# Result chains of a seven-product stage spread over successive slots, and two outputs of the last group taken together

## Chip, cores and metric

The kernel runs on one core of one Trainium2 chip. The core has TensorE (PE, matrix products), VectorE (DVE), ScalarE (ACT), GpSimd (POOL) and SyncE (SP, which only issues DMAs here), each with a queue of its own that it works through in order. The metric is the device time in microseconds of one execution; lower is better.

## The reference, cut to what matters

An attention layer with mixing of heads before and after the softmax feeds two multilayer blocks on 1792 tokens of width 768. The stages that matter here, called layers one to four:

```python
a = x @ w1                       # layer one, 768 -> 1024
b = x @ w2
y = (a * b @ w3) @ w_out         # layer two; the kernel multiplies by w3 @ w_out, 1024 -> 768
h = np.maximum(y @ w_in, 0.0)    # layer three, 768 -> 2048
out = h * h @ w_out2             # layer four, 2048 -> 768
```

## The kernel before, in words

The tokens are worked in two halves of 896, each half as two tiles t = 0, 1 of 448 tokens. Every float32 operand is split in a high and a low part, and each product is three matmuls (high by high, high by low, low by high; `mm3`, line 60). So every weight piece is prepared by ACT (`wh`, the rounded copy, line 117) and then by POOL (`wl`, the rest, line 145), and every activation by ACT (`...h`, line 711) and then DVE (`...l`, line 712).

All weight pieces form one list, and `stage(s, run)` is one slot of it. In slot s it issues, in this order: the DMA of a later piece, sums of weights for a piece further on (`combine`, DVE), `wh` of piece s+3, `wl` of piece s+2, then whatever earlier slots left in the list `late`, and then `run`, which is the matmuls of piece s and the work on their result. The program order of every engine is the order of these calls; nothing reorders it later. SP runs ahead of the others and waits only for the four buffers `raw`/`quad` of weights. What stands in `late[0]` is issued in the next slot, in `late[1]` in the one after, and so on.

In the second half of the tokens, layers one and three work two output blocks of 128 and both tiles together as one "quad": seven products of half depth instead of eight, in seven slots of nine matmuls each (`quad`, `l1_quad`, `l3_quad`). Four of the weight pieces are sums and differences, made by `combine` 1 to 4 (tiles S1 to S4). The products go to four PSUM banks A to D, some added onto an older result, in the order A, B, C, A, B, C, D. In slot 0 ACT copies A (`s1`); in slot 1 DVE adds `u2`; in slot 2 ACT copies C (`s5`). The four results (r, t) come out in slots 3 to 6: (0,0) by ACT's Relu in slot 3; (1,1) in slot 4, where DVE adds `u3` and then POOL adds u3 and s5; (0,1) in slot 5 and (1,0) in slot 6, added by DVE. Each result of layer three is then squared (DVE), rounded (ACT) and its rest taken (DVE): the "result chain". Quad j makes blocks 2j and 2j+1 of h.

Layer three and four alternate in the second half: quads 0, 1, 2, part 0, quads 3, 4, part 1, quads 5, 6, part 2, quad 7, part 3. A part gr of layer four (`l4_part`) multiplies blocks 4gr to 4gr+3 of h with the weights of the six outputs e = 0 to 5, one weight piece (one slot) for each output, 24 matmuls per slot, so that part 3 alone needs the results of the quad just ahead of it. Quad 7 (`end`) and the last quad of layer one use DVE in place of POOL for result (1,1).

In the tables below a matmul of layer four reads `l<-h_0h,wl` (tile 0, high part, low weights), and the suffixes of `qh4D` say quad 4 of layer three, bank D.

Of the kernel before, what the change touches and what calls it, by code (L numbers as in the profile page):

```python
# [14 lines left out]
ALU = mybir.AluOpType  # L15
# [22 lines left out]
def fused_kernel(ctx, tc, q, k, v, w_pre, w_post, w1, w2, w3t, wo, win, wo2, eye, out):  # L38
# [492 lines left out]
    class Moe:  # L531
        def __init__(self, pre):
            self.w = Weights(None, pre, PW, 4, 2, 3, 8, 8)
            self.wp, self.pre = None, pre
            self.xy, self.late, self.acc, self.ready = {}, [[] for _ in range(4)], {}, set()
            self.units, self.wot = [], {}
            for hf in range(2):
# [17 lines left out]
                if hf == 0:  # L555
                    for gr in range(2):
                        self.units += [self.l3(hf, 8 * gr + f) for f in range(8)]
                        self.units += [self.l4(hf, gr, e) for e in range(6)]
                else:
                    for gr in range(4):  # L560
                        js = range(2 * gr + (gr > 0), min(2 * gr + 3, 8))
                        self.units += [self.l3_quad(j) for j in js]
                        self.units += [self.l4_part(gr, e) for e in range(6)]
# [13 lines left out]
        def stage(self, s, run=None):  # L577
# [7 lines left out]
            if quad(s + 5) and self.pieces[s + 5][2] == ("S", 2, 0):  # L585
                w.combine(quad(s + 5), 1)
                w.combine(quad(s + 5), 2)
            if quad(s + 3):
                _, q, name = self.pieces[s + 3]
                if name[0] == "S" and name[1] > 2:  # L590
                    w.combine(q, name[1])
                w.ft[s + 3] = q.f[name]
                w.place(s + 3)
                w.high(s + 3)
# [228 lines left out]
        def l1_quad(self, j, second):  # L823
            end = j == 3

            def done(r, t, x, y=None):
# [10 lines left out]
                p = self.tile(f"p1_{m}_{t}")  # L837
                if y is not None:
                    self.add(p, x, y, eng)
                    x = p  # L840
                mul = lambda: nc.vector.tensor_tensor(p, x, self.xy["a", m, t], ALU.mult)
                if eng is nc.gpsimd:
                    self.late[0].append(mul)
                    self.split_late(ab, p, 1, 2)
                else:
                    mul()
                    self.split_late(ab, p, 0, 0 if end else 1)
# [4 lines left out]
        def l3_quad(self, j):  # L852
            end = j == 7

            def done(r, t, x, y=None):
                f = 2 * j + r
                eng = nc.gpsimd if r and t and not end else nc.vector
                hb = self.xy["h", 1, f, t] = self.pair(f"h1_{f}_{t}")
                p = self.tile(f"h21_{f}_{t}")
                if y is None:  # L860
                    nc.scalar.activation(p, x, AF.Relu)
                    nc.vector.tensor_tensor(p, p, p, ALU.mult)
                    self.split_late(hb, p)
                    return
                self.add(p, x, y, eng)
                square = lambda: nc.vector.scalar_tensor_tensor(p, p, 0.0, p, ALU.max, ALU.mult)
                if eng is nc.gpsimd:
                    self.late[0].append(square)
                    self.split_late(hb, p, 1, 2)
                else:  # L870
                    square()
                    self.split_late(hb, p, 0, 0 if end else 1)
# [120 lines left out]
        def l4_part(self, gr, e):  # L993
            def run(ws, _):
                accs = [self.psum(f"l41_{gr}_{e}_{t}") for t in range(2)]
                term = lambda c, t: (self.chunk(ws, c), self.xy["h", 1, 4 * gr + c, t])
                for cs, order in (((0, 1), (0, 1)), ((2,), (0, 1)), ((3,), (1, 0))):
                    for t in order:
                        mm3(accs[t], [term(c, t) for c in cs], cs[0] == 0, cs[0] == 3)
                for t, acc in enumerate(accs):  # L1000
# [11 lines left out]
            return [(wo2d[e, :, PW * gr : PW * gr + PW], False)], run  # L1012
# [123 lines left out]
```

## Time and profile before

| | us |
|---|---|
| median of 3 runs | 1320.99 (1317.67 to 1323.35) |
| profiled execution, its own time | 1316.99 |
| its span in the profile | 1314.9 |
| PE busy | 1274.1 (97%) |
| DVE busy | 835.6 (64%) |
| ACT busy | 707.1 (54%) |
| POOL busy | 528.3 (40%) |

The span runs from the first to the last recorded work; the device time has about 2 us more around it. PE is close to always busy, so the time that can be taken away without taking away matmuls is the little in which PE issues none or issues them slowly. Matmuls overlap, so idle time understates a stop: the distance from one start to the next is the safer measure. A share of busy time averages over stages; the rows below are from the stages that the change touches, from 900 us on.

### The profile page before, as it was taken

Reading aid. Unit: us, or ns where it says so; the run is one execution under the profiler, and the core shown is the slowest. Engines: PE = TensorE matmul, PEld = TensorE weight load, DVE = VectorE, ACT = ScalarE, POOL = GpSimd, SP = SyncE. Lnnn points to the kernel's source line nnn. Section 1 sums busy time; section 2 is a strip of 40 time slices with the busy share of each in tenths; the row PEclk is TensorE's granted clock in tenths of the full one; section 3 lists DMA queues with packets and bytes.
Section 4 is the critical chain, followed back from the end, with each engine's and each line's share of the span. In section 5 each row is a group of like instructions: output and inputs, shape, how many; then the busy total and the mean of one; then the engine's idle time right before and its main releaser. Section 6 shows DMA issues by size and latency. Waiting matters only on the chain.

```text
span 1314.9 us, 23201 instructions
## 1 busy us (share of the span) xinstructions
PE 1274.1 (97%) x8470; PEld 1096.2 (83%) x8470; DVE 835.6 (64%) x1520; ACT 707.1 (54%) x1565; POOL 528.3 (40%) x572
## 2 busy tenths in 40 slices
PE   7999999999998999999999999999999999999998
PEld 3667777776766798999999999999999998889897
DVE  5888888889788686543127734769666337364733
ACT  5988889888886565443225533544344334341420
POOL 4354265245324512002222322237676456453631
PEclk9999999999999999999999999999999999999999
DMA  6666476566566577654135744683221111211312
GB/s 216 167 179 190 132 202 207 140 186 202 143 176 195 159 218 224 218 157 150 65 93 156 209 159 131 177 293 122 80 73 57 61 52 44 77 47 52 87 32 84
DMA packets 105158, 184.50 MB, mean 140 GB/s; under 512 B 21589, under 2 KB 72789, under 8 KB 104533
## 3 DMA queue, kind: packets, MB, share of 16 engines
q1 hardware_dynamic: 84624, 160.40, 41.3%
q10 hardware_dynamic: 20421, 22.63, 4.8%
q8 instruction: 67, 1.10, 0.3%
q14 instruction: 46, 0.38, 0.1%
HBM read 111.43 MB, written 33.03 MB: 110 GB/s over the span
## 4 chain that ended last, share of the span: by engine, by line
PE 76%; DVE 6%; issue 6%; POOL 5%; DMA 4%; ACT 2%; SPq 0%; POOLq 0%; ACTq 0%; DVEq 0%
PE l L60 32%; PE sp L318 8%; PE y L60 7%; PE tp L383 5%; PE p L60 5%; PE pv L435 5%; POOL wl L145 4%; PE sc L292 4%; DMA r<-s 2%; DVE pl L374 2%; DMA kraw<-k 1%; DVE nm L324 1%; DVE p L397 1%; ACT ph L358 0%; DMA raw<-wo2d 0%
## 5 line engine op out<-in xcount | busy, mean ns | idle before, releaser
L145 POOL TENSOR_TENSOR wl<-f,wh 128x384 fp32r<-128x384 f32 (+1 forms) x88 | 101.0, 1149 | 309.7 <-ACT wh L117 299.6
L318 PE MATMUL sp<-r,kpre 120*120 120x448 f32 x360 | 159.2, 562 | 11.4 <-ACT p L332 7.3
L332 ACT ACTIVATE p<-sp,nm 120x448 f32<-120x448 f32 x180 | 113.8, 644 | 49.6 <-DVE nm L324 49.5
L374 DVE SCALAR_TENSOR_TENSOR pl<-p,sm,ph 120x448 f16<-120x448 f32 (+3 forms) x270 | 136.9, 561 | 0.0
L324 DVE TENSOR_REDUCE nm<-sp 120x1 f32<-120x448 f32 x180 | 107.7, 619 | 41.7 <-PE sp L318 37.4
L383 PEld LDWEIGHTS <-ph 120*128 120x128 f16 x1260 | 92.9, 98 | 31.6 <-issue 23.8
L101 DVE TENSOR_SCALAR f<-y 128x384 int32<-128x384 int32 (+1 forms) x120 | 82.5, 688 | 55.5 <-ACT y L89 53.6
L358 ACT ACTIVATE ph<-p,sm 120x448 f16<-120x448 f32 (+1 forms) x180 | 108.0, 666 | 16.8 <-DVE sm L352 12.6
L383 PE MATMUL tp<-kwh,ph 120*128 120x120 f16 x630 | 106.0, 217 | 4.8 <-DVE p L399 2.2
L347 POOL TENSOR_SCALAR sm<-sm 120x2 f32<-120x2 f32 (+3 forms) x94 | 25.0, 266 | 204.1 <-ACT p L332 200.1
L318 PEld LDWEIGHTS sp<-r,kpre 120*120 120x120 f32 x360 | 58.1, 183 | 56.3 <-issue 20.9
L383 PE MATMUL tp<-kwh,pl 120*128 120x120 f16 x630 | 105.1, 216 | 0.0
L383 PE MATMUL tp<-kwl,ph 120*128 120x120 f16 x630 | 105.1, 216 | 0.0
L292 PE MATMUL sc<-kt,qh 128*110 128x448 f32 (+1 forms) x192 | 98.2, 512 | 2.3 <-DVE kt L256 1.5
L303 ACT ACTIVATE s<-sc 110x448 f32<-110x448 f32 (+1 forms) x186 | 90.8, 561 | 5.5 <-PE sc L292 5.1
L145 POOL TENSOR_TENSOR wl<-raw,wh 128x512 fp32r<-128x512 f32 x48 | 66.4, 1392 | 50.8 <-ACT wh L117 50.2
L103 DVE SCALAR_TENSOR_TENSOR f<-raw,f 128x384 int32<-128x384 int32 (+1 forms) x120 | 81.4, 678 | 4.1
L117 ACT ACTIVATE wh<-f 128x384 fp32r<-128x384 f32 (+1 forms) x104 | 58.3, 561 | 43.5 <-DVE f L103 36.7
L435 PE MATMUL pv<-p,v 128*64 128x110 f32 (+1 forms) x1536 | 81.0, 262 | 0.6 <-ACT xs L445 0.6
L435 PEld LDWEIGHTS pv<-p,v 128*64 128x64 f32 x1536 | 74.1, 137 | 4.0 <-ACT xs L445 0.9
L60 PE MATMUL l<-h_0h,wl 128*128 128x448 f32 x192 | 70.0, 364 | 5.5 <-POOL wl L145 5.5
L397 DVE TENSOR_SCALAR p<-tp,iv 128x360 f32<-128x360 f32 x135 | 74.2, 578 | 1.3 <-PE tp L383 1.3
(1372 smaller groups left out, 3681.8 us busy)
## 6 DMA issues: line engine op xcount, KB each, us to landing
r<-s SPq DMA_DIRECT2D x172, 210.0 KB
raw<-w SPq DMA_DIRECT2D x32, 384.0 KB
raw<-win SPq DMA_DIRECT2D x32, 384.0 KB
raw<-wo SPq DMA_DIRECT2D x24, 512.0 KB
kraw<-k SPq DMA_DIRECT2D x24, 448.0 KB
raw<-w3t SPq DMA_DIRECT2D x16, 512.0 KB
qraw<-q SPq DMA_DIRECT2D x35, 220.0 KB
v<-v SPq DMA_DIRECT2D x4, 1536.0 KB
```

The costliest lines, as they stand in the source:

```text
L60: nc.tensor.matmul(acc, w, x, start=(first and i == 0 and j == 0), stop=(last and i == n - 1 and j == 2), skip_group_check=again,)
L145: eng.tensor_tensor(self.out[i][1], self.ft.pop(i), f32(self.out[i][0]), ALU.subtract)
L292: nc.tensor.matmul(sc[:ic], t[:, hh * ic : hh * ic + ic], self.kt[b, h // 2][:, h % 2], start=(i == 0), stop=(i == 1))
L303: nc.scalar.activation(self.st[n][:ic, h], self.sc.pop((n, h))[:ic], AF.Copy)
L318: nc.tensor.matmul(t[:kk], self.kpre[:kk, :kk], self.rt.pop(g)[:kk], start=True, stop=True)
L324: nc.vector.tensor_reduce(nm[:kk], self.sp[g][:kk], AX.X, ALU.max, negate=True)
L332: nc.scalar.activation(p[:kk], self.sp.pop(g)[:kk], AF.Exp, bias=self.nm.pop(g)[:kk], accum_out=self.sm[g // 2][:kk, g % 2 : g % 2 + 1],)
L358: nc.scalar.activation(h[:, to], p[:, fr], AF.Copy, scale=sm)
L374: nc.vector.scalar_tensor_tensor(l[:, to], p[:, fr], sm, h[:, to], ALU.mult, ALU.subtract)
L383: nc.tensor.matmul(t[:, j], p[:, at : at + 128], w, start=(i == 0), stop=(i == 2))
L397: nc.vector.tensor_scalar(d, t[:, main], self.iv, None, ALU.mult)
L435: nc.tensor.matmul(t[64 * e : 64 * e + 64, x, :w], self.v[b][:, j, g], self.p2[n][:, j * NH + g, :w], start=(j == 0), stop=(j == JC - 1),)
```

## The change

Four edits. The sums S3 and S4 of every quad are issued one slot earlier, in the slot ahead of the one in which ACT first reads them. The result chains are cut into links that are issued in successive slots: for the result (1,1) that POOL adds, the addition, the product or square, the rounding and the rest stand in the next slot and the three after it; for the other results of layer three outside the last quad, square, rounding and rest follow one slot apart; result (0,0) is cut so in the last quad too. And in part 3 the first two outputs of layer four form one unit of two slots: nothing is multiplied in the first, both are multiplied in the second, going through the blocks of h in the outer loop and the outputs in the inner one.

```diff
--- before.py
+++ after.py
@@ -532,7 +532,7 @@
         def __init__(self, pre):
             self.w = Weights(None, pre, PW, 4, 2, 3, 8, 8)
             self.wp, self.pre = None, pre
-            self.xy, self.late, self.acc, self.ready = {}, [[] for _ in range(4)], {}, set()
+            self.xy, self.late, self.acc, self.ready = {}, [[] for _ in range(5)], {}, set()
             self.units, self.wot = [], {}
             for hf in range(2):
                 if hf == 0:
@@ -560,7 +560,8 @@
                     for gr in range(4):
                         js = range(2 * gr + (gr > 0), min(2 * gr + 3, 8))
                         self.units += [self.l3_quad(j) for j in js]
-                        self.units += [self.l4_part(gr, e) for e in range(6)]
+                        es = [(e,) for e in range(6)] if gr < 3 else [(0, 1), (2,), (3,), (4,), (5,)]
+                        self.units += [self.l4_part(gr, x) for x in es]
             kept = [u[2] if len(u) > 2 else None for u in self.units]
             self.units = [u[:2] for u in self.units]
             self.pieces = [s for ss, _ in self.units for s in ss]
@@ -585,10 +586,10 @@
             if quad(s + 5) and self.pieces[s + 5][2] == ("S", 2, 0):
                 w.combine(quad(s + 5), 1)
                 w.combine(quad(s + 5), 2)
+            if quad(s + 4) and self.pieces[s + 4][2] in (("S", 3, 0), ("S", 4, 0)):
+                w.combine(quad(s + 4), self.pieces[s + 4][2][1])
             if quad(s + 3):
                 _, q, name = self.pieces[s + 3]
-                if name[0] == "S" and name[1] > 2:
-                    w.combine(q, name[1])
                 w.ft[s + 3] = q.f[name]
                 w.place(s + 3)
                 w.high(s + 3)
@@ -835,16 +836,16 @@
                     return
                 ab = self.xy["ab", 1, m, t] = self.pair(f"ab1_{m}_{t}")
                 p = self.tile(f"p1_{m}_{t}")
+                mul = lambda: nc.vector.tensor_tensor(p, x if y is None else p, self.xy["a", m, t], ALU.mult)
+                if eng is nc.gpsimd:
+                    self.late[0].append(lambda: self.add(p, x, y, eng))
+                    self.late[1].append(mul)
+                    self.split_late(ab, p, 2, 3)
+                    return
                 if y is not None:
-                    self.add(p, x, y, eng)
-                    x = p
-                mul = lambda: nc.vector.tensor_tensor(p, x, self.xy["a", m, t], ALU.mult)
-                if eng is nc.gpsimd:
-                    self.late[0].append(mul)
-                    self.split_late(ab, p, 1, 2)
-                else:
-                    mul()
-                    self.split_late(ab, p, 0, 0 if end else 1)
+                    self.add(p, x, y)
+                mul()
+                self.split_late(ab, p, 0, 0 if end else 1)
 
             src = [w12d[int(second), 2 * j + r] for r in range(2)]
             return self.quad(f"{j}{int(second)}", src, lambda: self.xq, 3, done)
@@ -854,22 +855,25 @@
 
             def done(r, t, x, y=None):
                 f = 2 * j + r
-                eng = nc.gpsimd if r and t and not end else nc.vector
                 hb = self.xy["h", 1, f, t] = self.pair(f"h1_{f}_{t}")
                 p = self.tile(f"h21_{f}_{t}")
+                square = lambda: nc.vector.scalar_tensor_tensor(p, p, 0.0, p, ALU.max, ALU.mult)
                 if y is None:
                     nc.scalar.activation(p, x, AF.Relu)
-                    nc.vector.tensor_tensor(p, p, p, ALU.mult)
-                    self.split_late(hb, p)
-                    return
-                self.add(p, x, y, eng)
-                square = lambda: nc.vector.scalar_tensor_tensor(p, p, 0.0, p, ALU.max, ALU.mult)
-                if eng is nc.gpsimd:
+                    self.late[0].append(lambda: nc.vector.tensor_tensor(p, p, p, ALU.mult))
+                    self.split_late(hb, p, 1, 2)
+                elif end:
+                    self.add(p, x, y)
+                    square()
+                    self.split_late(hb, p, 0, 0)
+                elif r and t:
+                    self.late[0].append(lambda: self.add(p, x, y, nc.gpsimd))
+                    self.late[1].append(square)
+                    self.split_late(hb, p, 2, 3)
+                else:
+                    self.add(p, x, y)
                     self.late[0].append(square)
                     self.split_late(hb, p, 1, 2)
-                else:
-                    square()
-                    self.split_late(hb, p, 0, 0 if end else 1)
 
             src = [wind[2 * j + r] for r in range(2)]
             return self.quad(f"h{j}", src, lambda: self.yq, 3, done)
@@ -990,14 +994,17 @@
             dst = wo2d[e, :, o : o + 1024]
             return [(wo2[e, :, o + PW * i : o + PW * i + PW], True) for i in range(2)], run, (dst, PW)
 
-        def l4_part(self, gr, e):
-            def run(ws, _):
-                accs = [self.psum(f"l41_{gr}_{e}_{t}") for t in range(2)]
-                term = lambda c, t: (self.chunk(ws, c), self.xy["h", 1, 4 * gr + c, t])
+        def l4_part(self, gr, es):
+            def run(ws, s):
+                if s + 1 < len(es):
+                    return
+                accs = {(e, t): self.psum(f"l41_{gr}_{e}_{t}") for e in es for t in range(2)}
                 for cs, order in (((0, 1), (0, 1)), ((2,), (0, 1)), ((3,), (1, 0))):
-                    for t in order:
-                        mm3(accs[t], [term(c, t) for c in cs], cs[0] == 0, cs[0] == 3)
-                for t, acc in enumerate(accs):
+                    for w, e in zip(ws, es):
+                        for t in order:
+                            terms = [(self.chunk([w], c), self.xy["h", 1, 4 * gr + c, t]) for c in cs]
+                            mm3(accs[e, t], terms, cs[0] == 0, cs[0] == 3)
+                for (e, t), acc in accs.items():
                     if gr == 0:
                         o = self.xy["o", e, t] = self.tile(f"oa1_{e}_{t}")
                         nc.scalar.activation(o, acc, AF.Copy)
@@ -1009,7 +1016,7 @@
                         self.add(o, acc, self.xy["o", e, t])
                         nc.sync.dma_start(out[e, :, HT + t * TB : HT + (t + 1) * TB], o)
 
-            return [(wo2d[e, :, PW * gr : PW * gr + PW], False)], run
+            return [(wo2d[e, :, PW * gr : PW * gr + PW], False) for e in es], run
 
     with tc.manual_schedule(), ExitStack() as base:
         sa, sb, sps = ExitStack(), ExitStack(), ExitStack()
```

On each engine the number of instructions stays as it was. Three places in their order. POOL, at the last slots of quad 2, just ahead of part 0 (wl220 belongs to the last piece of the quad, wl221 and wl222 to the first two outputs of part 0, h21_5_1 is result (1,1)), before:

```order
L145 TENSOR_TENSOR wl218_13407<-Sh23_13404,wh218_13406 128x384
L145 TENSOR_TENSOR wl219_13428<-Sh24_13425,wh219_13427 128x384
L145 TENSOR_TENSOR wl220_13446<-quadh21_13242,wh220_13445 128x384
L782 TENSOR_TENSOR h21_5_1_13484<-u3h2_13480,s5h2_13441 128x448
L145 TENSOR_TENSOR wl221_13466<-raw221_13402,wh221_13465 128x512
L145 TENSOR_TENSOR wl222_13489<-raw222_13423,wh222_13488 128x512
L145 TENSOR_TENSOR wl223_13514<-raw223_13443,wh223_13513 128x512
```

and now:

```order
L145 TENSOR_TENSOR wl218_13406<-Sh23_13380,wh218_13405 128x384
L145 TENSOR_TENSOR wl219_13427<-Sh24_13403,wh219_13426 128x384
L145 TENSOR_TENSOR wl220_13446<-quadh21_13239,wh220_13445 128x384
L145 TENSOR_TENSOR wl221_13465<-raw221_13401,wh221_13464 128x512
L783 TENSOR_TENSOR h21_5_1_13482<-u3h2_13478,s5h2_13441 128x448
L145 TENSOR_TENSOR wl222_13486<-raw222_13424,wh222_13485 128x512
L145 TENSOR_TENSOR wl223_13511<-raw223_13443,wh223_13510 128x512
```

The addition of the result has moved behind the low weights of the first output; quads 0, 1 and 3 to 6 have the same exchange with the piece that follows them. DVE, from slot 3 of quad 0 of layer three into slot 1 of quad 1 (h21_0_0, h21_1_1, h21_0_1, h21_1_0 are the four results, h1_...l their low parts, Sh11 to Sh14 the sums of quad 1), before:

```order
L141 TENSOR_TENSOR Sh11_13157<-quadh11_13103 128x384
L141 TENSOR_TENSOR Sh12_13159<-Sh11_13157,quadh10_13101 128x384
L862 TENSOR_TENSOR h21_0_0_13176<-h21_0_0_13176 128x448
L712 TENSOR_TENSOR h1_0_0l_13175<-h21_0_0_13176,h1_0_0h_13174 128x448
L782 TENSOR_TENSOR u3h0_13194<-qh0B_13127,s1h0_13119 128x448
L866 SCALAR_TENSOR_TENSOR h21_1_1_13198<-h21_1_1_13198 128x448
L782 TENSOR_TENSOR h21_0_1_13216<-qh0C_13145,u2h0_13137 128x448
L866 SCALAR_TENSOR_TENSOR h21_0_1_13216<-h21_0_1_13216 128x448
L782 TENSOR_TENSOR h21_1_0_13237<-qh0D_13225,u3h0_13194 128x448
L866 SCALAR_TENSOR_TENSOR h21_1_0_13237<-h21_1_0_13237 128x448
L712 TENSOR_TENSOR h1_1_1l_13197<-h21_1_1_13198,h1_1_1h_13196 128x448
L712 TENSOR_TENSOR h1_0_1l_13215<-h21_0_1_13216,h1_0_1h_13214 128x448
```

and now:

```order
L141 TENSOR_TENSOR Sh11_13157<-quadh11_13103 128x384
L141 TENSOR_TENSOR Sh12_13159<-Sh11_13157,quadh10_13101 128x384
L863 TENSOR_TENSOR h21_0_0_13176<-h21_0_0_13176 128x448
L783 TENSOR_TENSOR u3h0_13192<-qh0B_13129,s1h0_13121 128x448
L783 TENSOR_TENSOR h21_0_1_13214<-qh0C_13145,u2h0_13139 128x448
L713 TENSOR_TENSOR h1_0_0l_13175<-h21_0_0_13176,h1_0_0h_13174 128x448
L860 SCALAR_TENSOR_TENSOR h21_1_1_13196<-h21_1_1_13196 128x448
L860 SCALAR_TENSOR_TENSOR h21_0_1_13214<-h21_0_1_13214 128x448
L783 TENSOR_TENSOR h21_1_0_13235<-qh0D_13223,u3h0_13192 128x448
L141 TENSOR_TENSOR Sh13_13241<-quadh10_13101,quadh11_13103 128x384
L860 SCALAR_TENSOR_TENSOR h21_1_0_13235<-h21_1_0_13235 128x448
L141 TENSOR_TENSOR Sh14_13262<-quadh10_13101,Sh12_13159 128x384
```

u3 and the sum of (0,1) now stand ahead of the low part of (0,0) and of the square of (1,1), which wait for ACT and POOL; the sums Sh13 and Sh14 come ahead of the low parts of the quad before. PE, in part 3 (l41_3_e_t is output e of tile t, h1_13 and h1_14 blocks 13 and 14, wh274 the weights of output 0 and wh275 of output 1), before:

```order
L60 MATMUL l41_3_0_1_14878<-h1_13_1h_14474,wh274_14804 128x448
L60 MATMUL l41_3_0_1_14878<-h1_13_1l_14475,wh274_14804 128x448
L60 MATMUL l41_3_0_1_14878<-h1_13_1h_14474,wl274_14805 128x448
L60 MATMUL l41_3_0_0_14877<-h1_14_0h_14797,wh274_14804 128x448
L60 MATMUL l41_3_0_0_14877<-h1_14_0l_14798,wh274_14804 128x448
L60 MATMUL l41_3_0_0_14877<-h1_14_0h_14797,wl274_14805 128x448
```

and now:

```order
L60 MATMUL l41_3_0_1_14882<-h1_13_1h_14472,wh274_14803 128x448
L60 MATMUL l41_3_0_1_14882<-h1_13_1l_14473,wh274_14803 128x448
L60 MATMUL l41_3_0_1_14882<-h1_13_1h_14472,wl274_14804 128x448
L60 MATMUL l41_3_1_0_14883<-h1_12_0h_14450,wh275_14826 128x448
L60 MATMUL l41_3_1_0_14883<-h1_12_0l_14451,wh275_14826 128x448
L60 MATMUL l41_3_1_0_14883<-h1_12_0h_14450,wl275_14827 128x448
```

Ahead of the first matmul on block 14 stand now 24 matmuls on blocks 12 and 13, where 12 stood.

## Rows read from the trace of the kernel before

**Rows 1.** Stretches by window: start:end, length, busy time per engine, clock.

```profile
900.00:1000.00 100.00, 100.00 (x500) 93.21 (x499) 67.22 (x92) 41.63 (x88) 73.63 (x62) 1.00 0.23 75
...
1100.00:1200.00 100.00, 95.32 (x461) 86.61 (x460) 52.53 (x69) 38.65 (x79) 53.66 (x44) 0.98 0.23 64
```

**Rows 2.** Waits of PE, 880 to 1315: sum, times, longest.

```profile
PE l L60 <- POOL wl L145: 5.5, 3, 1.8
...
PE qh1C L60 <- POOL wl L145: 0.3, 1, 0.3
```

**Rows 3.** PE timeline: first matmuls of stages, a late one, the last.

```profile
920.17 0.36 PE L60 MATMUL q00A<-x1h,wh 128*128 128x448 f32 x1
...
954.86 0.47 PE L60 MATMUL q10C<-x1h,wl 128*128 128x448 f32 x1
...
1021.58 0.36 PE L60 MATMUL y<-ab_1h,wh 128*128 128x448 f32 x1
...
1079.18 0.36 PE L60 MATMUL qh0A<-y_0h,wh 128*128 128x448 f32 x1
...
1310.26 0.36 PE L60 MATMUL l<-h_0h,wl 128*128 128x448 f32 x1
```

**Rows 4.** PE timeline at the start of part 1 of layer four.

```profile
1177.45 0.37 PE L60 MATMUL l<-h_0l,wh 128*128 128x448 f32 x1
1179.63 0.47 PE L60 MATMUL l<-h_0h,wl 128*128 128x448 f32 x1 [1.82 <-POOL wl L145]
1179.94 0.37 PE L60 MATMUL l<-h_0h,wh 128*128 128x448 f32 x1
```

**Rows 5.** Timelines of ACT, then DVE, then POOL before that matmul.

```profile
1173.95 0.63 ACT L117 ACTIVATE wh<-raw 128x512 fp32r<-128x512 f32 x1
...
1175.98 0.63 DVE L712 TENSOR_TENSOR h_0l<-h,h_0h 128x448 fp32r<-128x448 f32 x1 [0.65 <-ACT h_0h L711]
1176.52 0.62 DVE L782 TENSOR_TENSOR u3h<-qh4B,s1h 128x448 f32<-128x448 f32 x1
1178.39 1.67 DVE L866 SCALAR_TENSOR_TENSOR h<-h 128x448 f32<-128x448 f32 x1 [1.25 <-POOL h L782]
...
1177.22 1.14 POOL L782 TENSOR_TENSOR h<-u3h,s5h 128x448 f32<-128x448 f32 x1 [2.37 <-PE qh4D L60]
1178.32 2.90 POOL L145 TENSOR_TENSOR wl<-raw,wh 128x512 fp32r<-128x512 f32 x2
```

**Rows 6.** Window just after: granted clock 0.50.

```profile
1181.20:1184.50 3.30, 3.30 (x10) 2.94 (x9) 3.27 (x4) 2.24 (x5) 3.21 (x3) 0.50 0.67 191
```

**Rows 7.** PE timeline, last group of layer four: first and last late matmul.

```profile
1281.43 0.36 PE L60 MATMUL l<-h_0h,wl 128*128 128x448 f32 x1
...
1286.25 0.36 PE L60 MATMUL l<-h_0h,wl 128*128 128x448 f32 x1
```

**Rows 8.** Timelines of DVE, then POOL at that group.

```profile
1278.02 0.63 DVE L866 SCALAR_TENSOR_TENSOR h<-h 128x448 f32<-128x448 f32 x1
...
1282.28 0.63 DVE L712 TENSOR_TENSOR h_1l<-h,h_1h 128x448 fp32r<-128x448 f32 x1 [0.64 <-ACT h_1h L711]
...
1283.48 1.14 DVE L866 SCALAR_TENSOR_TENSOR h<-h 128x448 f32<-128x448 f32 x1
1285.26 0.63 DVE L712 TENSOR_TENSOR h_0l<-h,h_0h 128x448 fp32r<-128x448 f32 x1 [0.64 <-ACT h_0h L711]
...
1279.86 1.30 POOL L145 TENSOR_TENSOR wl<-raw,wh 128x512 fp32r<-128x512 f32 x1 [2.35 <-ACT wh L117]
1282.85 1.29 POOL L145 TENSOR_TENSOR wl<-raw,wh 128x512 fp32r<-128x512 f32 x1 [1.69 <-ACT wh L117]
```

**Rows 9.** Windows: two quads of layer one; one of layer three.

```profile
945.38:970.77 25.39, 25.39 (x128) 23.54 (x126) 16.60 (x25) 10.82 (x23) 18.27 (x17) 1.00 0.20 63
...
1092.30:1106.60 14.30, 12.67 (x62) 11.07 (x61) 11.45 (x16) 6.73 (x14) 9.68 (x9) 1.00 0.10 25
```

**Rows 10.** Groups of DVE by form, 1079 to 1290: count | busy, mean ns.

```profile
L866 DVE SCALAR_TENSOR_TENSOR h<-h 128x448 f32<-128x448 f32 x24 | 26.3, 1097 | 9.4 <-POOL h L782 8.8
```

## The prediction

> **What bounds the kernel now.** I first read the busy time of the engines in stretches of 100 us, to see where PE is not full. From 900 to 1000 us, in the quads of layer one, it starts 500 matmuls in 100 us, so a 448-column matmul costs 0.200 us there; from 1100 to 1200 us, in layers three and four, only 461 are recorded [rows 1]. PE sets the time, and what can be gained is the distance from 0.200 us per matmul. The list of PE's waits then says who holds it: the largest entry is three waits of together 5.5 us for a low weight piece at the start of a part of layer four, and POOL is named [rows 2].
>
> Because matmuls overlap, idle time is less than what a stop costs, so I take the loss from starts. Layers three and four of the second half are 8 quads of 63 matmuls and 24 slots of 24, together 1080. Their first and last starts are 1079.18 and 1310.26 us [rows 3], 231.08 us apart; 1079 steps at 0.200 are 215.80. **15.28 us** are lost. The layer-one quads run from 920.17 to 1021.58 us [rows 3], 101.41 us for 504 matmuls, 100.80 at full pace: 0.61 lost. So 15.89 us bound the gain of anything that only removes PE's stops here.
>
> **The starts of the parts.** At part 1 the second matmul starts at 1177.45, the third at 1179.63 and the fourth at 1179.94 us [rows 4]: 2.49 us for two steps, 2.09 lost. The third is the first that needs the low weights. What holds them? ACT had rounded the piece by 1174.58 (1173.95 + 0.63), so the DMA had landed well before; POOL was idle from 1174.85 (2.37 us of idle time end at 1177.22), yet it did the piece only at 1178.32 [rows 5]. Ahead of it in POOL's queue stood the addition of result (1,1). That waited for u3 on DVE, which began at 1176.52, itself behind a low part that had waited 0.65 us for ACT [rows 5]. The line of POOL names a matmul as releaser; the value it needs is u3, ending 1177.14, 0.08 us before it starts.
>
> With the change the piece stands ahead of the addition. By the same rows POOL is free at 1174.85; 1.45 us (half of 2.90 for two) bring it to 1176.3, 1.3 us before the third matmul's due start at 1177.65. The loss goes whole. Behind the addition now stand the second output's weights: u3 1177.14, addition 1.14, piece 1.45, so about 1179.8, while PE takes 24 × 0.200 = 4.8 us for the first output and wants them after 1182. Parts 0 and 2 have the same three engines in the same order, and the three waits have one maximum, 1.8, with the sum 5.5 [rows 2]: 3 × 2.09 = **6.27 us**.
>
> **The half clock.** After the stop at part 1 PE's granted clock is 0.50, the lower level of 1.2 GHz, from 1181.2 to 1184.5 us: 10 matmuls in 3.30 us in place of 2.0 [rows 6], 1.3 us lost. Before the fall PE had lost the 2.09 us above. The other two stops of this size show no fall. I count **1.3 us** as gained, since the stop goes; the bounds are 0, if the fall was not its doing, and 1.3.
>
> **The last group.** In part 3 the loss lies between the starts at 1281.43 and 1286.25 us [rows 7], nine steps, 4.82 − 1.80 = **3.02 us**. Here quad 7's results are needed at once. 1281.43 is the fifteenth start of the part (twelve on blocks 12 and 13, three on block 14), so the part began at 1278.63. Now 24 matmuls on blocks 12 and 13 come first, so block 14 is due at 1283.43 for tile 0 and 1284.03 for tile 1, block 15 at 1285.83 and 1286.43. In the old order the low part of 14, tile 1, ends at 1282.91 and the last, of block 15, at 1285.89 [rows 8]. All are in time, the last by 0.5 us, even if the chains ran as before; they should be earlier, since u3 no longer stands behind the low part of (0,0). The weights of output 1 must be there at 1281.03 already; POOL had begun output 2's at 1279.86 [rows 8], so they are. If that reserve of 0.5 us fails, the price is what the last chain is late by, at most 3.02.
>
> **The seams between quads, and the sums.** The rest of the 15.28, 15.28 − 6.27 − 1.3 − 3.02 = 4.69 us, is spread over quads 0 to 2, 4 and 6: first pieces of the next quad behind POOL's addition, and pieces made from S4, whose sum reaches DVE late. The first kind goes by the exchange above. The second goes if one slot, 1.8 us (nine matmuls), is enough; such a wait, of bank C's second piece in quad 1, was 0.3 us [rows 2], so it is. The 0.61 us of layer one I count to the second kind: the late start is the first low weights of a C piece, at 954.86 us [rows 3], and layer one has three such stops of 0.19. In quad 0 the sums come right behind layer two's last work on DVE and cannot come earlier; I leave 0.2 us there and 0.3 us for seams I have not seen: **4.8 us** of 5.30.
>
> **What is added.** No engine has one instruction more, no DMA is added, and SP's order is the same. Waits move: the square of (1,1) on DVE waited 1.25 us for POOL [rows 5] and now comes two slots after u3; the result tiles are held up to two slots longer, which nobody waits for, as h is read by a part at least one quad later, except in part 3. I price both at nothing; the cover is the quad between (12.6 us), and without it each late link would cost up to the 1.25 us that the square waited.
>
> Sum: 6.27 + 1.3 + 3.02 + 4.8 = **15.4 us**. The profiled execution took 1316.99 us for a span of 1314.9; it should come to 1301.6. The median of the runs shown is 1320.99, 4.0 above it, so I forecast **1305.6 us**.
>
> **The rivals.** *DVE becomes the bound* (slower). A quad of layer three has 16 DVE instructions, and 12 of them (four squares, four low parts, four sums) read two operands from SBUF. A square took 0.63 us while POOL was idle and 1.14 us while POOL took a rest from 1282.85 on [rows 8]; the mean of 24 squares is 1.10 [rows 10]. If every one of the 12 now met POOL, a quad would need 16 × 0.63 + 12 × 0.5 = 16.1 us of DVE against 12.6 of PE, 3.5 too much, 28 us over eight quads; less the 15.9 that could be gained that is 12 us slower, 1333. It costs from 12.6 us of DVE on, and makes the kernel slower by 0.5% from about 15.4. Against it: quad 1 now holds DVE 11.45 us, such meetings included, and two quads of layer one with 25 DVE rows and 18.27 us of POOL run in 25.39 us with PE full [rows 9]. For it: the same work of POOL must now fit 12.6 us instead of 14.3. Chance 0.04. The Trainium skill says more strongly why such pairs cost: its page "SBUF — State Buffer", section "Who interferes with whom", states that a VectorE instruction with two SBUF inputs and a GpSimd instruction that reads SBUF exclude each other, the later one waiting for the whole of the earlier. By that rule alone all 12 could be hit, which gives this rival's 1333; the 0.63 and 1.14 above agree with it, the 11.45 says that few are hit.
>
> *A milder form*: DVE falls behind only in quads 0 to 2, and the seams' 4.8 us stay: 1310.4. Chance 0.10.
>
> *The low weights are held by their DMA*, so that the exchange on POOL moves nothing: 6.27 + 1.3 stay, 1313.2. Against it is the rounding on ACT, done 3.7 us before POOL's turn; it would need the loads, which wait for the sums to free a buffer, to come later, though the sums come earlier. Chance 0.05.
>
> *Nothing comes of it*, as a new stop of the same size takes the place of the old: 1321. The last reserve of 0.5 us is the only thin one, and it is worth 3.02. Chance 0.04.
>
> **How the numbers follow.** The forecast has the other 0.77, with its own range 1302 to 1309: the runs of before lie 5.7 us apart, and the clock's term may be 0. To hold 8 in 10 I go from 1300 to 1313, which takes in the milder form and nearly the DMA. No change is within 0.5%, 6.6 us, about what a measurement of this kernel can tell, that is down to 1314.4. Forecast, milder form and DMA lie below that, the last two by 4 us and 1.2 us, so I give part of them to no change: faster 0.88, same 0.08, slower 0.04.
>
> **What would show it.** In the profile of the changed kernel: 1080 matmuls from the first of quad 0 to the last in about 216.3 us; no wait of PE for `wl` at the third matmul of a part; on POOL the piece of a part's first output ahead of the addition; granted clock 1.00 throughout 1100 to 1200; in part 3 no wait for ACT or DVE. I am wrong if DVE shows no idle time in quads 1 and 2 and PE waits for weights made from sums there, or if PE waits in part 3 for block 15.

## The result, and the profile after

The changed kernel takes 1304.93 us (median of 4 runs, 1302.87 to 1307.36); the kernel before, run beside it, 1319.33 us (4 runs, 1316.81 to 1323.35). The ratio is 0.9889, 95% interval 0.9855 to 0.9923: faster by 1.1%. The forecast was 1305.6, in a range of 1300 to 1313.

The profiled execution of the changed kernel took 1307.36 us, its span 1305.3. First the same starts of matmuls as [rows 3], in PE's timeline of the changed kernel: layer one's quads, layer two, layer three's first quad, the last matmul.

```profile
921.65 0.36 PE L60 MATMUL q00A<-x1h,wh 128*128 128x448 f32 x1
...
1022.45 0.36 PE L60 MATMUL y<-ab_1h,wh 128*128 128x448 f32 x1
...
1080.05 0.36 PE L60 MATMUL qh0A<-y_0h,wh 128*128 128x448 f32 x1
...
1300.61 0.37 PE L60 MATMUL l<-h_0h,wl 128*128 128x448 f32 x1
```

Layers three and four now take 1300.61 − 1080.05 = 220.56 us; less 215.80 at full pace, 4.76 us are lost where 15.28 were. Layer one takes 100.80 us and loses nothing, where it lost 0.61. So 10.52 + 0.61 = 11.1 us came out of the stretches that the change touches, against 15.4 forecast. (The profile is 9.6 us shorter, not 11.1, as this execution reached layer one 1.48 us later, 921.65 against 920.17, after stages that the change leaves alone. That start varies: two more traces of the changed kernel have it at 917.25 and 919.81 us.) The list of PE's waits over these layers has four entries, none of them of before:

```profile
engine line waited for: us in total, times, longest us
PE qh1B L60 <- DVE u2h L783: 1.4, 1, 1.4
PE qh2B L60 <- DVE u2h L783: 1.0, 1, 1.0
PE qh6B L60 <- ACT h L862: 0.7, 1, 0.7
PE qh4B L60 <- ACT h L862: 0.7, 1, 0.7
```

The stops at the parts, in part 3 and at first and C pieces [rows 2, 4, 7] are gone. The windows by stretch (as in [rows 1]: length, then busy time of PE, its weight loads, DVE, ACT and POOL, then the granted clock) show the clock at its upper level, 2.4 GHz, from 1000 us on, and the 100 us from 1100 on with 483 matmuls where 461 were recorded:

```profile
1000.00:1100.00 100.00, 100.00 (x501) 93.33 (x499) 49.45 (x67) 42.91 (x85) 58.34 (x49) 1.00 0.18 57
1100.00:1200.00 100.00, 96.95 (x483) 90.25 (x483) 59.41 (x73) 37.16 (x75) 53.23 (x43) 1.00 0.22 62
```

At the start of part 1, PE's timeline of the changed kernel runs on at 0.20 us through the third matmul, and POOL's has the weight piece ahead of the addition, 1170.70 against 1173.11, as forecast (before: [rows 4, 5]):

```profile
1175.88 0.36 PE L60 MATMUL l<-h_0l,wh 128*128 128x448 f32 x1
1176.08 0.36 PE L60 MATMUL l<-h_0h,wl 128*128 128x448 f32 x1
...
1170.70 1.31 POOL L145 TENSOR_TENSOR wl<-raw,wh 128x512 fp32r<-128x512 f32 x1 [0.33 <-ACT wh L117]
1173.11 1.17 POOL L783 TENSOR_TENSOR h<-u3h,s5h 128x448 f32<-128x448 f32 x1 [1.10 <-DVE u3h L783]
```

The new stop is at the second B piece of a quad (slot 4, counted from 0), which adds onto bank B and so must wait until `u2` has been read out of it. In quad 1 it is the largest. PE's, DVE's and POOL's timelines there:

```profile
1099.67 0.37 PE L60 MATMUL qh1A<-y_0h,wl 128*128 128x448 f32 x1
1101.45 0.44 PE L60 MATMUL qh1B<-yT30h,wh 128*128 128x448 f32 x1 [1.41 <-DVE u2h L783]
...
1096.21 0.83 DVE L141 TENSOR_TENSOR Sh<-quadh,quadh 128x384 f32<-128x384 f32 x1
1096.97 0.61 DVE L860 SCALAR_TENSOR_TENSOR h<-h 128x448 f32<-128x448 f32 x1
1097.51 0.55 DVE L141 TENSOR_TENSOR Sh<-quadh,Sh 128x384 f32<-128x384 f32 x1
1097.98 2.79 DVE L713 TENSOR_TENSOR h_1l<-h,h_1h 128x448 fp32r<-128x448 f32 x2
1100.69 0.61 DVE L783 TENSOR_TENSOR u2h<-qh1B,s1h 128x448 f32<-128x448 f32 x1
...
1097.74 2.54 POOL L145 TENSOR_TENSOR wl<-Sh,wh 128x384 fp32r<-128x384 f32 x2 [1.11 <-ACT wh L117]
```

From 1099.67 to 1101.45 are 1.78 us for one step, 1.58 lost. DVE works without a pause, and ahead of `u2` stand the two sums S3 and S4 and two low parts of quad 0, which take 2.79 us for two while POOL takes two rests at the same time. Quads 2, 4 and 6 lose 1.14, 0.84 and 0.84: 4.4 of the 4.76.

For quads 4 and 6 the list of waits names ACT's Relu of result (0,0) in place of `u2`. PE's, DVE's and ACT's timelines in quad 4:

```profile
1169.15 0.37 PE L60 MATMUL qh4A<-y_0h,wl 128*128 128x448 f32 x1
1170.19 0.44 PE L60 MATMUL qh4B<-yT30h,wh 128*128 128x448 f32 x1 [0.67 <-ACT h L862]
...
1169.43 0.61 DVE L783 TENSOR_TENSOR u2h<-qh4B,s1h 128x448 f32<-128x448 f32 x1
...
1169.56 0.54 ACT L862 ACTIVATE h<-qh4A 128x448 f32<-128x448 f32 x1 [0.85 <-PE qh4A L60]
```

Both end here at nearly the same time, `u2` at 1170.04 and the Relu at 1170.10. PE starts 0.15 us after the end of `u2`, as it does in quad 1 (1101.30, 1101.45); and in the first kernel of the experiments below it starts this piece at 1163.40, ahead of the Relu at 1163.60. So it is `u2` in all four quads.

The windows of quads 1 and 2 show how full DVE is there (third busy time): 13.96 of 14.26 us and 12.77 of 13.82.

```profile
1092.67:1106.93 14.26, 12.85 (x64) 11.74 (x63) 13.96 (x18) 6.86 (x14) 10.94 (x9) 1.00 0.15 37
1106.93:1120.75 13.82, 12.85 (x64) 11.73 (x63) 12.77 (x14) 7.28 (x14) 11.58 (x10) 1.00 0.22 59
```

### The profile page after: what moved, and what is told of

Its sections match the earlier page's. It is cut to its first block, busy times and chain, and to the rows that moved or that the text cites. A ratio compares the mean times of both kernels' runs of the same rounds, so it can differ in the third digit from the quotient of the medians.

```text
span 1305.3 us, 23204 instructions
## 1 busy us (share of the span) xinstructions
PE 1270.1 (97%) x8470; PEld 1097.3 (84%) x8470; DVE 851.5 (65%) x1520; ACT 706.5 (54%) x1565; POOL 529.3 (41%) x572
## 5 line engine op out<-in xcount | busy, mean ns | idle before, releaser
L145 POOL TENSOR_TENSOR wl<-f,wh 128x384 fp32r<-128x384 f32 (+1 forms) x88 | 101.2, 1151 | 309.5 <-ACT wh L117 299.4
L145 POOL TENSOR_TENSOR wl<-raw,wh 128x512 fp32r<-128x512 f32 x48 | 64.8, 1360 | 56.6 <-ACT wh L117 52.9
L89 ACT ACTIVATE y<-raw 128x384 f32<-128x384 f32 (+1 forms) x120 | 69.8, 581 | 4.6 <-DMA raw<-wo 2.9
```

Source lines behind the costliest of these rows:

```text
L145: eng.tensor_tensor(self.out[i][1], self.ft.pop(i), f32(self.out[i][0]), ALU.subtract)
```

## Experiments

**Theory A**: the stop comes from the order on DVE. `u2` stands behind two low parts, which the earlier sums push to the moment at which POOL works on the rests of those sums, and there they run at half speed or less. **Theory B**: DVE simply has too much to do in a quad, and some piece is late in any order. Layers' losses below are worked out as above: starts apart, less full pace. "Beside" means on the same chip in the same series.

**One slot for two low parts.** One kernel issues the low parts of (1,1) (first pair of lines) and (0,1) (second) a slot later, behind `u2`; the other is the changed kernel again, as its measure.

```diff
-                    self.split_late(hb, p, 2, 3)
+                    self.split_late(hb, p, 2, 4)
...
-                    self.split_late(hb, p, 1, 2)
+                    self.split_late(hb, p, 1, 3 if t else 2)
```

> The changed kernel with one more edit: in layer three the low parts of results (1,1) and (0,1) are issued one slot later still, so that in slot 1 of the next quad DVE finds only S4 and u2. Loss means the time from the first matmul of quad 0 of layer three to the last matmul, less 1079 x 0.200 = 215.8 us; it was 15.28 before and is 4.76 in the changed kernel, of which 4.64 are four stops at bank B's second piece (slot 4) of quads 1, 2, 4 and 6. Theory A: these stops come from the order on DVE, u2 behind two low parts that are slowed by POOL. Then u2 is 2 to 3 us earlier, the four stops go, the loss is 0 to 0.5 us and the profile about 4.5 us shorter than that of the changed kernel in this stretch. Theory B: DVE simply has too much work for a quad of 12.6 us. Then the two low parts only hold something else (u3, sums S1 and S2), PE waits there, and the loss stays between 3 and 6 us.

> The changed kernel once more, to be timed beside the others on one chip, and to see whether its four stops come again. Both theories: loss 4.3 to 5.2 us, stops at slot 4 of quads 1, 2, 4 and 6, time about 1.1% below before.

Measured: 1300.89 us (1299.56 to 1302.23), ratio to before 0.9863 (0.9845 to 0.988), and the changed kernel beside it 1304.43 (1302.91 to 1306.72), 0.9888 (0.987 to 0.9905). The loss is 0.49 us against 4.72. DVE's timeline in quad 1 with the low parts later:

```profile
1094.45 0.61 DVE L783 TENSOR_TENSOR u2h<-qh1B,s1h 128x448 f32<-128x448 f32 x1
1094.99 2.26 DVE L713 TENSOR_TENSOR h_1l<-h,h_1h 128x448 fp32r<-128x448 f32 x2
```

The low parts are still slow (2.26 us), but nobody waits for them. What is left, 0.46 us, is at the first B piece of quad 2. DVE's busy time is the same (851.8 us, 851.5 in the changed kernel), so the stops came from the order: theory B falls. It was nearer than these totals say, as the windows of quads 1 and 2 in this kernel show:

```profile
1089.13:1101.73 12.60, 12.60 (x64) 11.81 (x63) 12.51 (x16) 6.05 (x13) 9.28 (x8) 1.00 0.16 42
1101.73:1114.80 13.07, 12.88 (x65) 11.74 (x63) 13.07 (x15) 6.94 (x15) 10.87 (x9) 1.00 0.19 43
```

DVE is busy 12.51 of 12.60 us and then all of 13.07; what it could not do in quad 2 it does in part 0.

**Whose doing is it?** Four kernels each have one or two of the edits on the kernel before or take one out. The result chains alone, with all of the changed `done` of layers one and three, of which two places:

```diff
-                    self.add(p, x, y, eng)
...
+                    self.late[0].append(lambda: self.add(p, x, y, eng))
+                    self.late[1].append(mul)
+                    self.split_late(ab, p, 2, 3)
...
-                    nc.vector.tensor_tensor(p, p, p, ALU.mult)
-                    self.split_late(hb, p)
...
+                    self.late[0].append(lambda: nc.vector.tensor_tensor(p, p, p, ALU.mult))
+                    self.split_late(hb, p, 1, 2)
```

> The kernel before with only the links of the result chains in successive slots (layer one and three); S3 and S4 as before, part 3 as before. Theory A: the three stops at the starts of parts (6.27 us, and the half clock) and those at the first pieces of quads 1 and 2 go, as POOL's addition has moved; the 3.0 us of part 3 stay, and the stops at u2 appear as in the changed kernel or a little smaller, since no sum stands ahead of them: loss 8 to 9 us. Rival, that the sums were needed too for the starts of the parts (their loads wait for S4): the stops of about 2 us at the parts stay, loss above 12 us.

Part 3's first two outputs together, alone (`l4_part` as changed, and):

```diff
-self.units += [self.l4_part(gr, e) for e in range(6)]
+es = [(e,) for e in range(6)] if gr < 3 else [(0, 1), (2,), (3,), (4,), (5,)]
+self.units += [self.l4_part(gr, x) for x in es]
```

> The kernel before with only the first two outputs of part 3 taken together. If the 24 matmuls on blocks 12 and 13 cover quad 7's chains in their old order too, the 3.0 us of part 3 go and nothing else: loss 12.3 us, or 11 if the half clock does not come. If the chains' new order was needed, PE waits in part 3 for block 15 and the loss is above 13.

S3 and S4 one slot earlier, alone:

```diff
+            if quad(s + 4) and self.pieces[s + 4][2] in (("S", 3, 0), ("S", 4, 0)):
+                w.combine(quad(s + 4), self.pieces[s + 4][2][1])
             if quad(s + 3):
...
-                if name[0] == "S" and name[1] > 2:
-                    w.combine(q, name[1])
```

> The kernel before with only S3 and S4 one slot earlier. Theory: they mend the late C pieces alone, 0.6 us in layer one and about 1.5 us in layer three; the stops at first pieces, at the parts and in part 3 stay (11.9 us without the half clock): loss 11.9 us and up to 1.5 us more for each fall of the clock. Rival, that they also bring the stops at u2 by themselves: loss above 16 us with stops at slot 4.

And the changed kernel with just that taken back:

> The changed kernel with S3 and S4 issued where they were before. Theory C: the four stops at u2 come from the earlier sums, since with them POOL takes the rests of S3 and S4 just when DVE takes the two low parts ahead of u2 (2.8 us for both in the changed kernel, 1.15 us with the links alone). Then no stop at slot 4, loss 0.4 to 0.9 us (the 3.06 of the links alone without the 2.4 of part 3), and about 4 us less device time than the changed kernel. Rival: the earlier sums are needed once part 3 is mended, or for the C pieces of quads 1 and 2; then stops of 0.2 to 0.7 us at C pieces return and the loss is 1.5 us or more.

| kernel | us | layer one loses | layers three and four lose |
|---|---|---|---|
| before, profiled | 1316.99 | 0.61 | 15.28 |
| links alone | 1303.35 (1 run) | 0.00 | 3.06, of it 2.65 in part 3 |
| pair alone | 1317.48 (1 run) | 0.64 | 15.43, none in part 3 |
| sums alone | 1317.42 (1 run) | 2.13 | 12.88 |
| links and pair | 1303.89 (1302.0 to 1304.78) | 0.00 | 0.42 |
| changed (again) | 1304.43 (1302.91 to 1306.72) | 0.00 | 4.72 |

The rows come from two series, in which before stood at 1318.88 us (links, pair, changed) and at 1316.37 us (sums, links and pair), so the losses compare better than the times. Links and pair stood at 0.9906 (0.989 to 0.9923) of before.

Three of these expectations missed. The links alone were to bring the stops at `u2` and lose 8 to 9 us; they bring none. The pair alone was to lose 11 to 12.3 us, or more if PE had to wait for block 15; it never waits in part 3 and loses 15.43, from two more falls of the clock than before (next section). The sums alone were to mend the late C pieces and leave the other stops, 11.9 us and up to 1.5 for a fall of the clock; 12.88 with one fall fits that by luck, as they bring stops at `u2` and shorten those at the parts.

PE's waits in the kernel with the sums alone show the stop that the sums bring, in layer one too:

```profile
PE qh1B L60 <- DVE u2h L782: 1.0, 1, 1.0
PE qh2B L60 <- DVE u2h L782: 0.9, 1, 0.9
PE qh6B L60 <- DVE u2h L782: 0.7, 1, 0.7
PE qh4B L60 <- DVE u2h L782: 0.7, 1, 0.7
...
PE l L60 <- POOL wl L145: 0.7, 3, 0.2
...
PE q30B L60 <- DVE u L782: 0.5, 1, 0.5
```

Alone they shorten the three waits at the parts from 5.5 us [rows 2] to 0.7 and pay with seven new stops. POOL's order is the old one there, but at part 1 `u3` ends 2.1 us ahead of the time at which the third matmul is due, where before it was 0.5 us; about 0.8 of the difference is PE itself coming later out of quad 4. With the links, which remove the parts' stops anyway, little but the price is left: 0.42 us lost without the sums, 4.72 with them. In the kernel with links alone two low parts in the same place take 1.15 us and POOL is idle for most of that (DVE's timeline, then POOL's):

```profile
1095.36 1.15 DVE L712 TENSOR_TENSOR h_1l<-h,h_1h 128x448 fp32r<-128x448 f32 x2
1096.43 0.61 DVE L782 TENSOR_TENSOR u2h<-qh1B,s1h 128x448 f32<-128x448 f32 x1
...
1096.13 1.25 POOL L145 TENSOR_TENSOR wl<-Sh,wh 128x384 fp32r<-128x384 f32 x1 [1.65 <-PE qh1C L60]
```

**Is POOL what makes the low parts slow?** The changed kernel, in which POOL leaves out the 56 rests of the weights of layer three's quads (the third matmul reads the high weights once more); `skip` is set for these quads:

```diff
-            if i in self.ft:
+            if i in self.ft and skip:
+                self.ft.pop(i)
+                self.out[i] = self.out[i][0], self.out[i][0]
+            elif i in self.ft:
```

> The changed kernel, but POOL takes no rests of the weights in the quads of layer three (56 instructions left out; the third matmul of each triple reads the high weights again), so DVE meets POOL there only at the additions. Theory (contention for SBUF): the low parts take 0.63 us in place of about 1.2, squares likewise, u2 is in time, and the four stops at slot 4 go: loss 0 to 0.5 us. Rival (the order on DVE alone holds u2, whatever POOL does): the low parts take as long as in the changed kernel, and the four stops stay, loss about 4.7 us.

Measured: 1299.58 us (1 run), 0.01 us less than full pace, no wait of PE. In DVE's timeline the same two low parts take 1.16 us in place of 2.79, with DVE's order untouched:

```profile
1092.48 1.16 DVE L717 TENSOR_TENSOR h_1l<-h,h_1h 128x448 fp32r<-128x448 f32 x2
1093.79 0.62 DVE L787 TENSOR_TENSOR u2h<-qh1B,s1h 128x448 f32<-128x448 f32 x1 [0.16 <-ACT wh L117]
```

So theory A needs both of its halves: the order and the meeting with POOL. The Trainium skill's page "SBUF — State Buffer", section "Who interferes with whom", says that a VectorE instruction with two SBUF inputs and a GpSimd instruction that reads SBUF exclude each other; 2.79 against 1.16 agrees.

**POOL's place alone.** On the kernel before, only POOL's addition of result (1,1), and the links behind it, one slot later (the place in layer three; layer one has the same):

```diff
-                self.add(p, x, y, eng)
+                if eng is nc.gpsimd:
+                    self.late[0].append(lambda: self.add(p, x, y, eng))
+                else:
+                    self.add(p, x, y, eng)
...
```

> The kernel before with only POOL's addition of result (1,1) and what follows it one slot later, in layers one and three; all other chains, the sums and part 3 as before. Theory A: the exchange on POOL alone takes away the stops at the parts and at first pieces (6.27 and 2.7 us) and with them the half clock; the C pieces and the 3.0 of part 3 stay: loss 3 to 5 us. Rival: u3 is late in any case, behind the low part that waits for ACT, and the later pieces of POOL are held instead; loss above 8 us, with waits for low weights at second pieces.

Measured: 1304.3 us (1 run); layer one loses nothing, layers three and four 5.95 us. PE's waits over these layers:

```profile
PE l L60 <- ACT h_0h L711: 1.0, 1, 1.0
PE l L60 <- ACT h_1h L711: 0.5, 1, 0.5
PE qh1C L60 <- POOL wl L145: 0.2, 1, 0.2
PE l L60 <- DVE h_1l L712: 0.2, 1, 0.2
```

Of the 5.95, some 3 are part 3's own stop and 1.1 a stretch at half clock behind it, which puts the loss above the 3 to 5 expected; quads 1 and 2 lose 1.6 in small stops of at most 0.38. The parts and the first pieces of the quads run through. One exchange on POOL is worth 15.28 − 5.95 + 0.61 = 9.9 us, with one stretch at half clock in either execution. It is set against the 11.1 of the whole change, in which the sums' price of 4.3 is already taken off.

**Is it device time?** The two mends and the changed kernel beside each other: without the edit of the sums (links and pair once more), and without it but with the low parts later.

> The changed kernel, as the measure for the two runs beside it. Both theories: about 1304.5 us (1303 to 1307), with 4.7 us lost in layers three and four of the second half, at the same four second B pieces.

> The changed kernel without its edit of the sums (S3 and S4 in their old slot), beside it on one chip. Theory A (the sums that come earlier push the low parts and u2 back on VectorE, and that costs 4.7 us and brings nothing): 0.4 us lost in layers three and four, 4.3 us less device time, about 1300, a ratio to the changed kernel of 0.9967. Theory C (what is no longer lost in these layers is lost in the stages ahead or behind, since the loads of later pieces move with the sums): the same loss of 0.4 us but a device time within 1 us of the changed kernel.

> The changed kernel without its edit of the sums, and with the low parts of results (1,1) and (0,1) of layer three one slot later: both mends of the new stop at once. Theory A: they mend the same stop, so nothing adds up; 0.4 to 0.5 us lost, device time within 1 us of the kernel with either mend alone, about 1300. Rival: the low parts, a slot later, now meet the late sums on VectorE, and second C or B pieces wait, 0.3 to 0.6 us in each of quads 1, 2, 4 and 6, 1301 to 1302.

| kernel | us (beside before at 1318.25) | ratio to before | loses |
|---|---|---|---|
| changed | 1304.74 (1301.33 to 1305.74) | 0.9896 (0.9878 to 0.9915) | 4.74 |
| without the sums | 1301.39 (1298.8 to 1302.71) | 0.9877 (0.9858 to 0.9895) | 0.40 |
| without, low parts later | 1302.43 (1300.42 to 1303.15) | 0.9884 (0.9868 to 0.9901) | 1.28 |

The sums' 4.3 us show as 3.4 in the medians, for theory A and against the C of these runs (that the time is lost in other stages instead), though single runs of the two overlap. In the other series the same kernel stood at 0.9906 of before, no better than the changed kernel did in any series (0.9888 to 0.9896); so the loss is settled by the traces, and its size in device time rests on this one series. Both mends at once lose more than either: PE's only listed wait is `PE qh2B L60 <- POOL wl L145`, 0.7 us. The rival had low parts and sums meet on DVE, in four quads and at second pieces; they do meet, but in quad 2 alone, where the first B piece waits for the low weights of S2. In the timeline of that kernel ACT waits for this sum, which stands behind the low parts on DVE:

```profile
1101.34 0.53 ACT L117 ACTIVATE wh<-Sh 128x384 fp32r<-128x384 f32 x1 [3.64 <-DVE Sh L141]
```

The best version measured is thus the changed kernel with the low parts later (1300.89) or without the sums (1301.39, and 1303.89 in the other series); these two were not run beside each other.

## Why the prediction was right, and where its steps were not

**The starts of the parts** (6.27 us): right, in place, cause and size; POOL's addition moved alone removes them.

**The last group** (3.02): right. The pair alone takes away that stop and none of the others. The thin reserve was there: in the changed kernel the last low part ends at 1278.89, and its first reader starts 1.1 us later, where 0.5 was forecast (DVE's timeline, then PE's):

```profile
1278.26 0.63 DVE L713 TENSOR_TENSOR h_0l<-h,h_0h 128x448 fp32r<-128x448 f32 x1 [0.65 <-ACT h_0h L712]
...
1280.01 0.36 PE L60 MATMUL l<-h_0l,wh 128*128 128x448 f32 x1
```

**The seams and the sums** (4.8 of 5.30): the step that failed. The old stops did go, so the milder rival, in which they stay, is not what happened; but 4.76 us of new ones came, net 0.54. The milder rival's price of 4.8 us was paid all the same, through DVE falling behind as it has it, but at another place and in quads 4 and 6 too. Two statements were wrong. First, that the pieces made from S4 needed the sums earlier: layer one's 0.61 us vanish with the links alone, and of the C pieces some 0.2 us in quad 2 are left. Second, under "What is added", that the moved work costs nothing with "the cover is the quad between". I asked who waits for the results of the moved instructions, and not who stands behind them on DVE. Behind S3, S4 and the low parts stands `u2`, which is issued in slot 1 and which PE needs in slot 4. The warning that PE would wait in quads 1 and 2 if DVE had no idle time there came true in part: DVE idles 0.30 us in quad 1 and 1.05 in quad 2, and PE waits for a bank to be read out and not for weights. The bound of 1.25 us for a late link was worked out for another wait, and that it is near the sizes found (1.58, 1.14, 0.84, 0.84) is luck; the largest goes past it, and there are four.

**DVE as the bound** of the whole did not come, and the order on DVE decided. But what the rival rested on, meetings with POOL, was real, hit the two instructions that mattered, and filled DVE in quads 1 and 2 past the 12.6 us from which the rival said that it costs: 13.96 and 12.77 us of work in the changed kernel, against 8.74 and 7.71 where POOL's rests are left out. The 11.45 us that spoke against it were read from the old order.

**The half clock** (1.3): it went with the stop, as forecast, and was a little larger. Part 1 of before loses 3.69 us from its first start to the next stage's, parts 0 and 2 lose 2.10 each, so the fall cost 1.6; the other 0.3 stood among the seams, which leaves 0.2 as their net gain. For the median the term may be too small still. In the profile of before one stop of three was followed by a fall [rows 6]; in the kernel with the pair alone all three were. Its PE timeline at part 0, and the window behind, with a granted clock of 0.55:

```profile
1121.47 0.36 PE L60 MATMUL l<-h_0l,wh 128*128 128x448 f32 x1
1123.66 0.47 PE L60 MATMUL l<-h_0h,wl 128*128 128x448 f32 x1 [1.82 <-POOL wl L145]
...
1124.80 0.57 PE L60 MATMUL l<-h_1h,wh 128*128 128x448 f32 x1
1125.17 0.57 PE L60 MATMUL l<-h_1l,wh 128*128 128x448 f32 x1
```

```profile
1125.00:1128.00 3.00, 3.00 (x10) 2.67 (x10) 2.96 (x4) 1.67 (x3) 2.93 (x3) 0.55 0.59 171
```

Steps of 0.37 us in place of 0.20; the three parts lose 3.70, 3.70 and 3.67 us, 1.6 us more each than a part with the stop alone. That is why this kernel, with part 3 mended, loses as much as before. Other executions of before may have had several too: beside the changed kernel and the one with low parts later, seven of them ran from 1313.14 us at a granted clock of 0.999, averaged over the execution, to 1322.13 at 0.992, the changed kernel's four from 1302.91 at 0.999 to 1306.72 at 0.996. So the total came out right by luck, as two errors offset each other. In the profiled executions 11.1 us were gained, 6.3 + 3.0 + 1.6 + 0.2; the medians lie 1319.33 − 1304.93 = 14.4 apart. The other 3.3 would be two more falls of that size in a usual execution of before, and this is argued, not shown: only one execution of it was traced, the stages ahead vary by up to 4.4 us (917.25 to 921.65), and the clock falls in them too (0.50 from 28.6 to 31.8 and from 93.4 to 96.7 us in the profile after). The averages do not settle it. Where before and the changed kernel ran side by side, the clock averages 0.994 and 0.997 in one series, 0.995 and 0.998 in another; but without the sums, a kernel with no such stop either, it is 0.996 twice, beside 0.997 and 0.995 of before.

## What to carry to other kernels

Work that is issued earlier on an in-order engine delays everything behind it: for each moved instruction look up what now stands behind it and when that is wanted, not only who waits for its own result. When one exchange removes a row of stops (here POOL's addition behind the next weights, 9.9 us), the further edits should be costed against the kernel with that exchange, as the reason for them may be gone. Price an instruction at the speed it has beside its neighbour engine, not at its speed alone. And read an engine's fill from the stretch that matters: DVE is busy 65% of the changed kernel and 98% of quad 1.

## What the runs showed of the hardware

A low part of 128x448 takes 0.58 us where POOL is idle and about 1.4 us where POOL takes rests back to back (1.16 against 2.79 us for two; two squares met like this took 2.79 us as well), more than the 0.63 to 1.14 of the squares in [rows 8]. A stop of PE of about 2 us, not longer, was followed by a stretch at the lower clock, 1.2 GHz, in one case of three in one execution and in three of three in another; none followed the single stops of 1.6 us and less in the changed kernel. Behind part 3's stops, two of 0.6 to 1.2 us close together, it fell in two kernels (sums alone, POOL's addition alone) and not in two (before, links alone). What decides between them stays open.
